# Second expert layer in three exact passes over 12-bit parts, weights in quarters of an expert, two attention units in turn

## The chip, the cores and the metric

The kernel runs on one core of a Trainium2 chip. In it TensorE does the matmuls, VectorE and ScalarE the work element by element, and transfers between device memory and the core's own memory are issued from DMA queues. The profile also records which share of its full clock TensorE was granted; in these traces that is full or half. The metric is the device time of the program in microseconds (us).

## The reference, cut to what matters

```python
q, k, v, alpha: (4 batches, 8 heads, 768 rows, 48)            # attention
for t in range(S):
    state = alpha[:, :, t, :, None] * state + einsum('bhd,bhe->bhde', k[:, :, t], v[:, :, t])
    y[:, :, t] = einsum('bhd,bhde->bhe', q[:, :, t], state)
x = y as (3072, 384)                                           # bridge
p = probs / (probs.sum(-1, keepdims=True) + 1e-09)             # 4 experts
for e in range(E):
    h = np.maximum(x @ w1[e], 0.0)                             # first layer, 384 -> 1024
    out += p[:, e:e + 1] * (h @ w2[e])                         # second layer, 1024 -> 384
```

## The kernel before

The attention is cut into 24 units of 128 rows. The experts run over seven groups of units: groups 0 and 1 have two units, groups 2 to 6 four. An "up" is 128 hidden columns of the first layer for one group; a "down" is the second layer of one expert for one unit. From group 1 on an up is exact through three cheap passes over parts of 12 bits: the high parts are multiplied, the low parts, and the differences of the two, and the mixed terms follow by subtraction. The parts of the weights are made once, in group 0, and kept in device memory. The second layer is in full precision:

```python
for out, parts in ((one, (1, 0)), (two, (2,))):        # up, groups 1 to 6
    for part in parts:
        for kc in range(KC):
            nc.tensor.matmul(out, lhsT=w1t[i][:, part, kc, col], rhs=xTs[gi][:, part, kc, :n], ...)
...
for fc in range(FCH):                                  # down: 8 matmuls in full precision
    nc.tensor.matmul(ops, lhsT=hidden[gi, e, h][:, f, slot * P:(slot + 1) * P], rhs=w2[:, fc, :], ...)
```

Weights come in halves of an expert. In group 0 a raw half, its scratch and its parts lie in different tiles, so no load waits for a store out of the same tile:

```python
t = staged[i] = wts.tile([P, KC, FH], F32, name="w_raw")     # raw half, two buffers
...
w = wts.tile([P, 3, KC, FH], F32R, name="w1")                # its parts, two buffers
... ScalarE and VectorE make the parts ...
nc.sync.dma_start(out=kept[i], in_=w.bitcast(F32))
```

## Time and profile before

| | before |
|---|---|
| time, median of 4 runs beside the changed kernel | 1339.6 us (1339.1 to 1342.6) |
| TensorE idle, from the trace | 51 us |
| half clock: half of the busy time inside the half-clock intervals of the clock record | 51 us, 17 of it in the start |
| the rest: TensorE's work at full clock | 1236 us |

The three rows below the time add up to the profiled span.

### The profile page before, as it was taken

Reading aid. Unit: us, or ns where it says so; the run is one execution under the profiler, and the core shown is the slowest. Engines: PE = TensorE matmul, PEld = TensorE weight load, DVE = VectorE, ACT = ScalarE, POOL = GpSimd, SP = SyncE. Lnnn points to the kernel's source line nnn. Section 1 sums busy time; section 2 is a strip of 40 time slices with the busy share of each in tenths; the row PEclk is TensorE's granted clock in tenths of the full one; section 3 lists DMA queues with packets and bytes.
Section 4 is the critical chain, followed back from the end, with each engine's and each line's share of the span. In section 5 each row is a group of like instructions: output and inputs, shape, how many; then the busy total and the mean of one; then the engine's idle time right before and its main releaser. Section 6 shows DMA issues by size and latency. Waiting matters only on the chain.

```text
span 1338.6 us, 18141 instructions
## 1 busy us (share of the span) xinstructions
PE 1287.5 (96%) x7288; PEld 944.0 (71%) x7288; DVE 600.5 (45%) x1320; ACT 324.2 (24%) x669; POOL 2.5 (0%) x14
## 2 busy tenths in 40 slices
PE   7999998899999999999999999999999999999998
PEld 6777777777777676676766776766767767656665
DVE  7456645543553553544544535535435435211221
ACT  1333311221232131231221321312312213211221
POOL 0000000000000000000000000000000000000000
PEclk7689988887999999999999999999999999999999
DMA  9188865553562452444533625524435325335430
GB/s 229 30 310 279 336 231 177 156 189 117 187 214 62 152 182 78 165 134 126 190 106 107 212 60 177 165 95 166 142 118 189 123 76 186 118 127 203 150 110 24
DMA packets 147138, 207.38 MB, mean 155 GB/s; under 512 B 104944, under 2 KB 136816, under 8 KB 139888
## 3 DMA queue, kind: packets, MB, share of 16 engines
q1 hardware_dynamic: 143680, 206.06, 46.2%
q8 instruction: 58, 0.95, 0.3%
q10 hardware_dynamic: 3376, 0.17, 0.2%
q14 instruction: 24, 0.20, 0.0%
HBM read 182.62 MB, written 23.59 MB: 154 GB/s over the span
## 4 chain that ended last, share of the span: by engine, by line
PE 90%; DVE 5%; ACT 3%; issue 1%; DMA 0%; SPq 0%; DVEq 0%; ACTq 0%
PE ops L353 39%; PE hps L328 27%; PE sc L221 11%; PE yps L256 3%; PE hps L311 3%; PE sc L218 3%; PE tp L179 2%; PE yps L253 1%; PE sps L267 1%; ACT t L333 1%; ACT AT L192 1%; DVE hT L334 1%; DVE lat L243 1%; ACT hT L338 1%; DVE acc L361 0%
## 5 line engine op out<-in xcount | busy, mean ns | idle before, releaser
L353 PE MATMUL ops<-w,hT 128*128 128x384 f32 x1536 | 524.7, 497 | 3.7 <-DVE acc L361 3.2
L353 PEld LDWEIGHTS ops<-w,hT 128*128 128x128 f32 x1536 | 289.2, 192 | 197.4 <-issue 6.9
L328 PE MATMUL hps<-xT,w 128*128 128x512 f32 (+1 forms) x1728 | 412.8, 389 | 4.6 <-DVE xT L295 4.0
L328 PEld LDWEIGHTS hps<-xT,w 128*128 128x128 f32 x1728 | 305.2, 194 | 63.0 <-DVE xT L295 4.5
L333 ACT ACTIVATE t<-hps 128x512 f32<-128x512 f32 (+1 forms) x192 | 107.7, 561 | 482.9 <-PE hps L328 482.8
L334 DVE TENSOR_TENSOR hT<-t,hps 128x512 f32<-128x512 f32 (+1 forms) x192 | 123.2, 642 | 165.9 <-ACT t L333 114.6
L221 PEld LDWEIGHTS sc<-QT,KT 48*128 48x128 f32 x1920 | 141.6, 209 | 58.5 <-issue 55.5
L361 DVE SCALAR_TENSOR_TENSOR acc<-ops,p_all,acc 128x384 f32<-128x384 f32 x72 | 44.5, 617 | 297.7 <-PE ops L353 297.7
L221 PE MATMUL sc<-QT,KT 48*128 48x64 f32 x1920 | 158.8, 300 | 12.7 <-DVE lat L243 12.6
L235 ACT COPY lat<-sc 32x128 f32<-32x128 f32 (+1 forms) x144 | 39.7, 292 | 359.8 <-PE sc L218 357.7
L243 DVE COPY_PREDICATED lat<-masks,sc 128x256 f32<-128x256 uint8 x240 | 116.6, 555 | 0.0
L338 ACT ACTIVATE hT<-hT 128x512 f32<-128x512 f32 (+1 forms) x192 | 112.9, 588 | 7.1 <-DVE hT L334 6.9
L227 DVE TENSOR_TENSOR QT<-QT,dec 128x256 f32<-128x256 f32 x144 | 61.2, 425 | 64.8 <-PE sc L221 56.4
L228 DVE TENSOR_TENSOR KT<-KT,dec 128x256 f32<-128x256 f32 x144 | 60.2, 418 | 0.0
L358 DVE TENSOR_SCALAR acc<-ops,p_all 128x384 f32<-128x384 f32 x24 | 14.8, 618 | 97.2 <-PE ops L353 97.2
L256 PE MATMUL yps<-rv,lat 128*128 128x48 f32 x384 | 56.4, 278 | 0.0
L256 PEld LDWEIGHTS yps<-rv,lat 128*128 128x128 f32 x384 | 52.9, 204 | 0.2
L311 PE MATMUL hps<-xT,w_raw 128*128 128x256 f32 x192 | 50.6, 414 | 0.6 <-ACT xT L288 0.6
L218 PEld LDWEIGHTS sc<-QT,KT 48*96 48x96 f32 (+1 forms) x768 | 34.2, 155 | 22.2 <-issue 19.4
L311 PEld LDWEIGHTS hps<-xT,w_raw 128*128 128x128 f32 x192 | 38.0, 206 | 7.5 <-ACT xT L288 1.0
L218 PE MATMUL sc<-QT,KT 48*96 48x64 f32 (+1 forms) x768 | 40.5, 246 | 2.1 <-DVE dec L230 1.9
L258 DVE TENSOR_TENSOR own<-own,yps 128x384 f32<-128x384 f32 x24 | 13.3, 554 | 46.9 <-PE yps L256 46.9
(53 smaller groups left out, 537.6 us busy)
## 6 DMA issues: line engine op xcount, KB each, us to landing
w<-kept SPq DMA_DIRECT2D x48, 2304.0 KB, 9.0
w<-in_moe_w_dram SPq DMA_DIRECT2D x28, 1536.0 KB, 7.0
kept<-w SPq DMA_DIRECT2D x8, 2304.0 KB, 8.0
w_raw<-in_moe_w_dram SPq DMA_DIRECT2D x8, 768.0 KB, 9.7
ra<-in_alpha_dram SPq DMA_DIRECT2D x24, 192.0 KB, 6.6
rk<-in_k_dram SPq DMA_DIRECT2D x24, 192.0 KB, 4.3
rq<-in_q_dram SPq DMA_DIRECT2D x24, 192.0 KB, 4.1
rv<-in_v_dram SPq DMA_DIRECT2D x24, 192.0 KB, 3.4
```

The lines of the kernel that those rows point to most:

```text
L218: nc.tensor.matmul(sc[i][:P - m, p, :], lhsT=KT[rows, p, :P - m], rhs=qv[rows, p, :, 1, :], start=True, stop=True)
L221: nc.tensor.matmul(sc[i][:, p, :], lhsT=KT[rows, p, :], rhs=qv[rows, p, :, 1, :], start=True, stop=True)
L227: nc.vector.tensor_mul(qv[:, :, :, 1, :], qv[:, :, :, 1, :], spread(left))
L228: nc.vector.tensor_mul(kv[:, :, :, 0, :], kv[:, :, :, 0, :], spread(right))
L243: nc.vector.copy_predicated(halves(lat[:, i], m)[:, :, :, 1, :], mk.unsqueeze(1).broadcast_to([P, NP, nb, m]), sc[i].rearrange("p a (b r) ...
L256: nc.tensor.matmul(yps[:, p, i, :], lhsT=lat[:, i, p, :], rhs=rv[:, 2 * p + i, :], start=(cb == 0), stop=(cb == 0 or i == 1))
L311: nc.tensor.matmul(out, lhsT=staged[i][:, kc, f * P:(f + 1) * P], rhs=xTs[gi][:, kc, :], start=(kc == 0), stop=(kc == KC - 1))
L328: nc.tensor.matmul(out, lhsT=w1t[i][:, part, kc, col], rhs=xTs[gi][:, part, kc, :n], start=(part == parts[0] and kc == 0), stop=(part == p ...
L333: nc.scalar.activation(out=t, in_=one, func=ACT.Copy, scale=1 + 1 / 4096.0)
L334: nc.vector.tensor_sub(hT, t, two)
L338: nc.scalar.activation(out=r, in_=r, func=ACT.Relu)
L353: nc.tensor.matmul(ops, lhsT=hidden[gi, e, h][:, f, slot * P:(slot + 1) * P], rhs=w2[:, fc, :], start=(fc == 0), stop=(fc == FCH - 1))
```

## The change

The intent is to put the second layer, the dearest group of the profile, through the same three passes. Each down then has 24 cheap matmuls instead of 16 instructions of full precision. For that the hidden values and the second-layer weights need parts too. The weights of both layers now lie in quarters of an expert, and the parts are made in the buffer that the raw quarter was loaded into. There are four buffers for the second layer and three for the first. The attention is dealt out by estimated time, two units in turn. The order changes too: the kernel before runs the downs of one expert between the two halves of the next expert's ups, and the changed kernel runs all ups of an expert and then its downs.

```diff
+    split1 = lambda gi, e: gi > 0
+    split2 = lambda gi, e: gi > 1 or gi == 1 and e < E // 2
+    makes = {0: lambda gi, e: gi == 0,
+             1: lambda gi, e: gi == 0 and e < E // 2 or gi == 1 and e >= E // 2}
 [...]
+    def load_piece(l, i):
+        w = wt[l][i] = wts.tile([P, 3, KC * QF], F32R, name=f"w{l + 1}", bufs=3 if l == 0 else NQ)
+        if (split1, split2)[l](gi, e):
+            nc.sync.dma_start(out=w.bitcast(F32), in_=kept[l][k])
+        elif l == 0:
+            nc.sync.dma_start(out=w[:, 2]..., in_=moe_w1[e]...)
 [...]
+    def split_piece(l, i):                        # in place: the raw quarter lies in part 2
+        nc.scalar.activation(out=top, in_=dif.bitcast(F32), func=ACT.Copy, scale=TRIM)
+        nc.vector.tensor_sub(low.bitcast(F32), dif.bitcast(F32), top.bitcast(F32))
+        nc.scalar.activation(out=low, in_=low.bitcast(F32), func=ACT.Copy, scale=4096.0)
+    def keep_piece(l, i):
+        nc.vector.tensor_sub(dif, top.bitcast(F32), low.bitcast(F32))
+        nc.sync.dma_start(out=kept[l][i % (E * NQ)], in_=w.bitcast(F32))
 [... up: the hidden values are split too ...]
+            nc.vector.tensor_sub(t, t, two)
+            finish.append(split(t, parts, relu=True))      # ScalarE once, VectorE twice
 [... down ...]
+                nc.tensor.matmul(sums[0], lhsT=h[:, 1], rhs=w[:, 1], start=(fc == 0), stop=False)
+                nc.tensor.matmul(sums[0], lhsT=h[:, 0], rhs=w[:, 0], start=False, stop=(fc == FCH - 1))
+                nc.tensor.matmul(sums[1], lhsT=h[:, 2], rhs=w[:, 2], **ends)
 [... attention ...]
+                turn = waiting.pop(0)
+                if next(turn, waiting) is not waiting:
+                    waiting.insert(min(1, len(waiting)), turn)
+                    due -= 1.0
```

## The prediction

> **What bounds the kernel now.** I read the page's first two parts, the groups, the table of stretches and then the timelines. The program runs 24 attention units of 128 rows and an expert layer over seven groups of them: groups 0 and 1 hold two units, groups 2 to 6 four. While a group's experts run, TensorE also does the attention of the next group. Group boundaries below are the starts of each group's first matmul of the first layer.
>
> ```profile
> PE 1287.5 (96%) x7288; PEld 944.0 (71%) x7288; DVE 600.5 (45%) x1320; ACT 324.2 (24%) x669; POOL 2.5 (0%) x14
> PEclk7689988887999999999999999999999999999999
> DMA  9188865553562452444533625524435325335430
> ```
>
> The reader is to see that TensorE sets the time, and that the first quarter differs: there its clock is granted in part and the DMA engines are busiest. The table of stretches says it by stage (columns: length; busy us of each engine; granted clock; DMA share; GB/s):
>
> ```profile
> 0.00:52.00 52.00, 43.00 (x311) 39.33 (x311) 30.30 (x80) 9.06 (x21) 2.53 (x14) 0.65 0.61 152
> 52.00:165.00 113.00, 105.59 (x600) 80.01 (x601) 69.85 (x115) 41.55 (x68) 0.00 (x0) 0.95 0.77 273
> 165.00:341.00 176.00, 159.27 (x1070) 127.30 (x1070) 83.01 (x213) 36.60 (x103) 0.00 (x0) 0.84 0.52 174
> 540.00:750.00 210.00, 207.53 (x1196) 149.67 (x1197) 97.20 (x220) 49.00 (x102) 0.00 (x0) 0.99 0.42 137
> 1163.00:1338.00 175.00, 170.05 (x609) 114.33 (x607) 35.01 (x53) 37.39 (x67) 0.00 (x0) 1.00 0.37 131
> ```
>
> Group 3 (540 to 750) is TensorE and nothing else; DVE has 97 of 210 us. The costliest groups:
>
> ```profile
> L353 PE MATMUL ops<-w,hT 128*128 128x384 f32 x1536 | 524.7, 497 | 3.7 <-DVE acc L361 3.2
> L328 PE MATMUL hps<-xT,w 128*128 128x512 f32 (+1 forms) x1728 | 412.8, 389 | 4.6 <-DVE xT L295 4.0
> L361 DVE SCALAR_TENSOR_TENSOR acc<-ops,p_all,acc 128x384 f32<-128x384 f32 x72 | 44.5, 617 | 297.7 <-PE ops L353 297.7
> ```
>
> Of the second layer, 768 matmuls of the program are 1536 instructions. What one costs is read where nothing is mixed in, in the chain of waits of the last group, which has no attention (start, us, what):
>
> ```profile
> 1232.00 16.50 PE hps L328 x72
> 1248.50 20.64 PE ops L353 x64
> ```
>
> 64 instructions of 384 columns in 20.64 us are 322.5 ns each, so one row block of one expert ("down") costs 16 x 322.5 = 5.16 us. 72 reduced-precision matmuls of 512 columns in 16.50 us are 229 ns each, so one slice of 128 hidden columns ("up") costs 9 x 229 = 2.06 us. For 256 columns (group 1) the trace has 116 to 120 ns from start to start inside a run.
>
> **What the Trainium skill says.** "FP8 and Floating Point Precision", TensorE Precision Notes: "True FP32: 4 passes through PE array". The trace agrees: two instructions of 322.5 ns for 384 columns, and 2 x 384 cycles at the 2.4 GHz that "TensorE: Matmul & The Clock Gate" names are 320 ns. "VectorE: DVE Perf Modes", the perf-mode tier table: a two-tensor fp32 operation stays at 1x. It agrees: 128x512 took 686 ns, 128x256 422 ns, 128x1536 1756 ns, about 1.04 ns an element and 155 ns besides. "DMA: Bandwidth & Descriptors", Anatomy of one DMA: semaphore waits happen on the issuing sequencer, not in the DMA engines, so one wait holds everything issued behind it. The trace agrees: the waits of the DMA queue include 295.3 us of first-layer weight loads waiting for TensorE. "TensorE: Matmul & The Clock Gate", HAM oscillation: idle gaps over about 3.4 us return the array to half clock. The clock record of this trace knows only full and half, 106 us of half in all, 55 of them in group 1.
>
> **The change part by part.**
>
> *Second layer in three passes.* From group 2 on, and for two experts of group 1, a down becomes 24 single-instruction matmuls of 384 columns. No row shows that size; between 118 ns (256) and 229 ns (512) lies 173.5 ns, so 4.17 us. The saving is 0.99 us for each of 80 + 4 downs: 83 us, all on the path of TensorE. This is the whole direct gain, 6.2%.
>
> *What it adds on DVE.* Hidden values must be split: to the one subtraction of an up come two more two-tensor operations, 3 x 0.69 = 2.07 us an up against TensorE's 2.06. Each down has two accumulations of 0.617 us in place of one. So DVE is full in the up phases before any attention. From the built order I counted, in each up phase of eight, the attention work that stands in it, by the durations of the trace. TensorE then has 24.3, 26.3, 24.3 and 20.5 us in the four experts' up phases of a steady group; DVE has 32.3, 20.5, 31.8 and 23.5 us. PSUM (four banks, two for an up) lets TensorE lead by about two ups. At the end the split of the last slices must be finished before the first down reaches its last quarter, about 3.5 us in; DVE ends about 2.7 us after its own sum because of the first up and the first activation. So the stalls are 32.3 + 2.7 - 24.3 - 3.5 = 7, none, 7 less what the tail pieces give back, and 2: I take 13 us a group in groups 3 and 4, 10 in group 2, 15 in group 5, 3 in group 6, together 54. In the down phases DVE has about 13 of 23 us.
>
> *What it moves in DMA.* Second-layer parts are kept too: 24 stores of 1152 KB in group 0 (16 first layer, 8 second) and 8 in group 1. The parts now lie in the load's own buffer. So a load into it waits for the store out of it, and while the DMA queue waits for that nothing behind is issued. In the trace a store of 2304 KB has its first packet 0.8 us after issue, 8 packets of 0.80 us an engine, and lands 0.4 us later (8.0 in all). Half of it is 0.8 + 3.2 + 0.4 = 4.4 us. With the next load (384 KB, 1.1 us) ahead of the next store, a cycle is 5.45 us; with a load of 1152 KB (3.0 us by 0.37 us a packet) 7.3 us. First-layer weights have three buffers for four quarters. The fourth quarter of an expert therefore waits for the store of the first, and after an expert whose second layer was kept, that store stands behind four such cycles, 22 us. TensorE gets through three quarters in 10 to 12 us. Walking the queue's order with these numbers, group 0 stalls by 3, 14, 16 and 3 us (36); group 1 by 10 (three stores and four loads of group 0's end lie ahead), 2, 4 (this one DVE) and 16 (32); the first expert of group 2 by 17 (four cycles of 7.3 us, attention inputs, then its quarter). From then on the loads of an expert (4.7 MB, 11.8 us) and the fourth quarter (3.0) land about 14 us into an up phase of 24 that needs it after 18: hidden.
>
> *Attention dealt by time, two units in turn.* It takes away waits of TensorE for the attention chain, and by itself helps group 1, which now loses 22 us to gaps and 26 to half clock.
>
> **The sum.** TensorE's work at full clock after the change, from the built order and these durations: start 51, group 0 113, group 1 125, groups 2 to 4 186.5 each, group 5 177, group 6 133, together 1158. The same tally for the kernel before is 83 more, 1241, of its 1339; the other 98 are idle time (51, from the page) and half clock (about 50). After: 1158 + 36 + 32 + 17 for DMA + 54 for DVE + 22 for half clock after the long stalls (two thirds of what is lost now would be 33; some hides inside the stalls) = **1319 us**, 1.5% less.
>
> **Rivals.** (a) *TensorE stays the only bound*: the two units in turn hide DVE, the stores land earlier than I reckon, and of 83 us some 70 are kept and group 1 gains 20 more: about 1250. For it: before the change DVE delays TensorE by 3 us in the down groups; the down phases have DVE time to spare. Against it: DVE's 32 us in an up phase of 24, and no bank for TensorE to lead further. (b) *The DMA queue takes the start over entirely*: the stalls in groups 0 to 2 add a half clock each time and attention loads wait in the same queue: 1360 to 1380. For it: the DMA share in group 0 is already 0.77, and the bytes of groups 0 and 1 grow from some 60 to over 80 MB. (c) *DVE sets steady groups too*: more attention waits on a late DVE, a steady group stays at 208 as now; then 1319 + 20.
>
> **Range and chances.** The direct gain is certain within 10 us (the 384-column spacing). The DMA stalls are 85 with an error of 25, DVE's 54 with 20, the clock 22 with 15. Together some 37, so 1268 to 1366. My own sum stands just above the limit of 2% (1313), hence faster 0.44, same 0.46, slower 0.10; the last is (b).
>
> **What would show it.** In the changed profile: second-layer matmuls spaced 174 ns; steady groups about 200 us with DVE over 70% busy and waits of TensorE for the hidden tiles in the first and third expert; in groups 0 to 2 waits of TensorE for DMA into the first-layer weights of 10 to 17 us each, about six of them, each followed by half clock; no DMA wait after group 2. I am wrong if group 0 takes under 130 us, or steady groups take 188, or if DMA waits go on to the end.

## More of the kernel before

One more view of this kernel, the waits of TensorE (what waited and for what; us in total, times, longest):

```profile
PE tp L179 <- ACT AT L192: 14.8, 21, 2.0
PE sc L221 <- DVE lat L243: 12.6, 15, 2.2
PE tp L179 <- DMA ra<-in_alpha_dram: 4.2, 2, 3.6
```

TensorE's longest wait is 3.6 us, and it never waits for a weight.

## The result, and the profile after

The changed kernel takes 1420.4 us (median of 4 runs, 1417.3 to 1428.4) against 1339.6: slower by 6.1%, ratio 1.0607 with a 95% interval of 1.056 to 1.0655. Ratios here are the mean time of one kernel's fast runs over that of the other's fast runs of the same rounds, so they are not quite the ratio of the medians quoted. All outputs are right. The prediction, 1319 us, was wrong, and its range, up to 1366, did not hold the result.

First the page of the changed kernel, the lines that answer to the three at the head of the prediction:

```profile
PE 1254.8 (88%) x7960; PEld 1090.6 (77%) x7960; DVE 850.5 (60%) x1744; ACT 376.5 (27%) x759; POOL 2.5 (0%) x14
PEclk7677879578576879999999999999999999999999
DMA  6276466957335765647655735846466575367663
```

TensorE has less to do, 1254.8 us for 1287.5, and the span is 81 us longer. The loss lies in the first 15 of the 40 slices, 533 us, where the clock is granted in part. The table of stretches puts figures on it (columns as in the prediction; group 0, 1, 2, a steady group, the last group):

```profile
54.00:257.00 203.00, 135.80 (x686) 101.58 (x686) 85.15 (x157) 60.18 (x110) 0.00 (x0) 0.79 0.61 212
257.00:461.00 204.00, 170.09 (x1058) 149.45 (x1059) 99.02 (x241) 51.72 (x123) 0.00 (x0) 0.70 0.57 199
461.00:688.00 227.00, 198.26 (x1334) 174.37 (x1333) 142.77 (x296) 56.34 (x113) 0.00 (x0) 0.93 0.61 206
688.00:888.00 200.00, 196.09 (x1328) 173.28 (x1327) 140.17 (x291) 55.33 (x111) 0.00 (x0) 0.97 0.60 210
1276.00:1420.00 144.00, 133.81 (x672) 120.34 (x670) 81.68 (x126) 38.54 (x68) 0.00 (x0) 1.00 0.62 245
```

A steady group takes 200 us where it took 210: that part of the change works. Group 0 takes 203 where 113 were needed before, and group 1 takes 204 for 176. The waits of TensorE in the changed kernel:

```profile
PE one L343 <- DMA w<-kept: 50.2, 7, 22.9
PE one L335 <- DMA w<-in_moe_w_dram: 47.5, 4, 19.4
PE sc L241 <- DVE lat L254: 26.0, 15, 6.7
PE sc L238 <- ACT lat L247: 10.8, 19, 3.8
```

The first two did not exist before: the first layer waits for its weights. There are four such waits in group 0 (5.3, 19.4, 16.7 and 6.2 us), a long one in group 1 (20.0) and one in the first expert of group 2 (22.9), 90.5 us together; five more, 0.9 to 2.4 us, stand in group 6. The other two are attention; four of these, 3.4 to 6.7 us, fall in the downs of group 0. There the chain's own VectorE and ScalarE work stands behind the making of weight parts.

The chain of work that ended last, in the stretch of the 19.4 us wait (start, us, what):

```profile
98.91 8.05 DMA kept<-w
...
107.49 6.08 DMA kept<-w
...
114.08 5.89 DMA kept<-w
...
120.48 5.76 DMA kept<-w
...
126.29 4.75 DMA w<-in_moe_w_dram
```

The reader sees four stores one behind the other, the four second-layer quarters of the first expert. Behind them stands the load of the first-layer quarter that TensorE is waiting for. The load into a quarter's buffer must wait for the store out of it, and the DMA queue issues nothing past that wait.

The account of the two traces, by my sum over the matmuls and the clock record (us; idle / half clock / work at full clock):

| | before | after |
|---|---|---|
| whole span | 51 / 51 / 1236 | 165 / 105 / 1150 |
| group 0 of the changed kernel | | 67 / 22 / 114 |
| group 1 | | 34 / 50 / 120 |
| group 2 | | 29 / 5 / 193 |
| group 3 | | 4 / 5 / 191 |

So 86 us of TensorE's work are gone, and they are given back by 114 us more idle time and 53 us more half clock.

### The profile page after: what moved, and what is told of

The parts are those of the page before. It is cut to its first block, busy times and chain, and to the rows that moved or that the text cites. A ratio compares the mean times of both kernels' runs of the same rounds, so it can differ in the third digit from the quotient of the medians.

```text
span 1420.0 us, 20156 instructions
## 1 busy us (share of the span) xinstructions
PE 1254.8 (88%) x7960; PEld 1090.6 (77%) x7960; DVE 850.5 (60%) x1744; ACT 376.5 (27%) x759; POOL 2.5 (0%) x14
## 4 chain that ended last, share of the span: by engine, by line
PE 69%; DVE 13%; DMA 11%; ACT 2%; issue 2%; SPq 1%; DVEq 0%; ACTq 0%
PE one L343 14%; PE ops L390 9%; PE ops L391 8%; PE ops L393 8%; PE sc L241 7%; PE two L343 6%; DMA kept<-w 5%; DMA w<-kept 4%; DVE lat L254 3%; PE yps L275 3%; PE sc L238 3%; PE one L335 3%; PE ops L395 3%; PE tp L197 2%; PE yps L272 2%
## 5 line engine op out<-in xcount | busy, mean ns | idle before, releaser
L343 PE MATMUL one<-xT,w 128*128 128x512 f32 (+1 forms) x1152 | 304.6, 403 | 50.4 <-DMA w<-kept 50.2
L343 PEld LDWEIGHTS one<-xT,w 128*128 128x128 f32 x1152 | 210.2, 203 | 91.0 <-issue 48.0
L347 ACT ACTIVATE t<-one 128x512 f32<-128x512 f32 (+1 forms) x192 | 108.1, 563 | 548.5 <-PE one L343 481.5
L390 PE MATMUL ops<-w,hT 128*128 128x384 f32 x672 | 236.1, 351 | 0.0
L393 PE MATMUL ops<-w,hT 128*128 128x384 f32 x672 | 230.3, 343 | 0.0
L391 PE MATMUL ops<-w,hT 128*128 128x384 f32 x672 | 230.1, 342 | 0.0
L349 DVE TENSOR_TENSOR t<-t,two 128x512 f32<-128x512 f32 (+1 forms) x176 | 116.3, 661 | 101.0 <-PE two L343 74.0
L343 PE MATMUL two<-xT,w 128*128 128x512 f32 (+1 forms) x576 | 161.1, 391 | 0.0
L343 PEld LDWEIGHTS two<-xT,w 128*128 128x128 f32 x576 | 111.6, 205 | 20.5
L179 DVE SCALAR_TENSOR_TENSOR hT<-hT 128x512 fp32r<-128x512 f32 (+1 forms) x176 | 117.5, 668 | 6.1
L175 DVE SCALAR_TENSOR_TENSOR hT<-t,hT 128x512 fp32r<-128x512 f32 (+1 forms) x176 | 116.0, 659 | 0.0
L172 ACT ACTIVATE hT<-t 128x512 fp32r<-128x512 f32 (+1 forms) x176 | 106.3, 604 | 9.6 <-DVE t L349 9.6
L335 PEld LDWEIGHTS one<-xT,w 128*128 128x128 f32 x192 | 44.9, 243 | 58.0 <-issue 31.5
```

Source lines behind the costliest of these rows:

```text
L172: nc.scalar.activation(out=top, in_=x, func=ACT.Relu if relu else ACT.Copy, scale=TRIM)
L175: nc.vector.scalar_tensor_tensor(out=low, in0=x, scalar=0.0, in1=top.bitcast(F32), op0=ALU.max, op1=ALU.subtract)
L179: nc.vector.scalar_tensor_tensor(out=dif, in0=top.bitcast(F32), scalar=1 / 4096.0, in1=low.bitcast(F32), op0=ALU.mult, op1=ALU.subtract)
L335: nc.tensor.matmul(one, lhsT=w[:, 2, kc].bitcast(F32), rhs=xraws[gi][:, kc, :n], start=(kc == 0), stop=(kc == KC - 1))
L343: nc.tensor.matmul(out, lhsT=w[:, part, kc], rhs=xTs[gi][:, part, kc, :n], start=(part == terms[0] and kc == 0), stop=(part == terms[-1] a ...
L347: nc.scalar.activation(out=t, in_=one, func=ACT.Copy, scale=FINE)
```

## The experiments

Three theories. A: the DMA queue and the missing fourth buffer of the first layer. B: in group 1 the mix of short matmuls keeps the clock at half after it has once fallen. C: attention held behind the weights' making on VectorE and ScalarE. The rival to all of them was the plain sum of bytes and VectorE work, whatever its order. A table of all stages follows the last run; medians of the kernel before were 1337.7 to 1338.0 us.

**Second-layer transfers on a queue of their own.**

```diff
-            nc.sync.dma_start(out=w.bitcast(F32), in_=kept[l][k])
+            (nc.sync, nc.gpsimd)[l].dma_start(out=w.bitcast(F32), in_=kept[l][k])
   (the raw second-layer load and the store likewise)
```

> All loads and stores of second-layer weights are issued from GpSimd's queue instead of SyncE's; nothing else changes. Theory A (TensorE's long waits for a first-layer quarter come from the one in-order DMA queue, where the second layer's store-then-load cycles stand ahead; and these waits set off most of the half clock): the seven waits over 5 us (sum about 114 us in the changed kernel) fall to under 40 us, busy time at half clock in groups 0 to 2 falls from 155 us to under 90, total about 1310 to 1330. Theory B (the waits cost only themselves; the half clock of group 1 comes from its mix of 256-column ups with small attention matmuls): idle falls by the same 60 to 75 us, but group 1 still has about 80 to 100 us busy at half clock, total 1345 to 1360. Theory C (the splits of weights in the in-order queues of ScalarE and DVE hold everything up): waits hardly change, total within 20 us of 1420.

1411.0 us, ratio 1.055 (1.0508 to 1.0592). The first-layer waits shrink: 5.5, 11.1, 12.7 and 6.0 us in group 0, 5.1 in group 1, none in group 2. In their place TensorE waits for second-layer quarters, 6.5 + 4.0 us in group 1 and 8.4 + 7.1 in group 2. Idle falls by 20 us, half clock rises by 10. By the medians the order in one queue is worth 9 us, not 80, and the two intervals overlap. By time this is the branch of theory C, though the waits did change. The edit also changes the kind of queue: the page of this run has 132 MB under a software queue, where the changed kernel has almost all under one hardware queue.

**The second layer in full precision everywhere.**

```diff
-    split2 = lambda gi, e: gi > 1 or gi == 1 and e < E // 2
+    split2 = lambda gi, e: False
-             1: lambda gi, e: gi == 0 and e < E // 2 or gi == 1 and e >= E // 2}
+             1: lambda gi, e: False}
```

> The second layer stays in full precision everywhere, no parts of it are made, stored or loaded; quarters, attention by time and the two units in turn stay. Its matmuls cost 84 x 0.99 = 83 us more. Theory A: without second-layer stores the waits for quarters shrink to under 25 us in all and the half clock to the level of the kernel before (some 65 us busy at half), total about 1335, i.e. the kernel before again. Theory B: waits go too, but group 1 keeps half clock in its ups (80 us busy at half or more), total about 1365 to 1385. Theory C: like A for the waits; TensorE's waits for attention in group 0's down phases (19 us) go as well.

1373.4 us, ratio 1.0267 (1.0219 to 1.0314). Without its three-pass second layer the change is still 2.7% slower than before; the first-layer waits of group 0 are then 4.2 to 6.1 us each. So the second layer in parts costs another 47 us net, and 36 come from the rest. The time lies in the range of theory B, but its reason does not hold here. Group 1:

```profile
210.00:364.00 154.00, 144.43 (x1031) 117.36 (x1030) 72.03 (x191) 39.42 (x108) 0.00 (x0) 0.89 0.60 195
```

Its ups and its attention are those of the changed kernel, and theory B expected 80 us or more of busy time at half clock there; 33 us were recorded. The half clock costs group 1 16 us here, 50 in the changed kernel and 26 in the kernel before.

**Ups of group 1 run twice** (the same result written again).

```diff
-            for out, terms in ((one, (1, 0)), (two, (2,))):
+            for out, terms in ((one, (1, 0)), (two, (2,))) * (2 if gi == 1 else 1):
```

> In group 1 alone each up runs its nine matmuls twice (the second run overwrites the first, the result is the same): 288 more matmuls of 118 ns, 34 us at full clock, 68 at half. Theory A (waits set off the half clock): group 1 gets longer by 34 to 60 us, total 1450 to 1480. Theory B (too little dense work between attention pieces keeps the clock at half): the up phases of group 1 run at full clock (3.1 us a slice instead of 4.1), busy time at half clock in group 1 falls from 100 us to under 50, and in spite of more work the total is 1385 to 1420.

1429.5 us, ratio 1.0676 (1.0644 to 1.0708). TensorE gets 37 us more work at full clock in group 1, yet the stage grows only from 204.5 to 209.0 us. The stretch of group 1 in this run:

```profile
257.00:466.00 209.00, 176.86 (x1348) 159.61 (x1348) 99.06 (x242) 52.23 (x124) 0.00 (x0) 0.88 0.55 194
```

The granted clock rises from 0.70 to 0.88 and the busy time at half clock falls from 101 to 39 us. Much of group 1's time is the low clock, which long runs of matmuls lift: that part of theory B holds. Its range for the time, 1385 to 1420, was missed by 9 us. Two stretches of group 1 in the changed kernel show what it looks like (after the length: busy us of TensorE; the first 0.50 is the clock):

```profile
253.00:294.00 41.00, 39.14 (x218) 36.31 (x219) 26.47 (x71) 5.62 (x16) 0.00 (x0) 0.50 0.86 298
342.00:379.00 37.00, 36.60 (x209) 32.61 (x208) 19.77 (x54) 6.76 (x18) 0.00 (x0) 0.50 0.46 162
```

TensorE is recorded busy for 95 and 99% of these stretches and stays at half clock for 41 and 37 us. The matmuls of 256 columns in them come 214 ns apart, against 116 to 120 ns at full clock, so the record is right here. Between the ups stand bursts of 16 attention matmuls of 64 columns.

**The parts made just before their store instead of ahead of use.**

```diff
     def keep_piece(l, i):
+        split_piece(l, i)
   (the two earlier calls of split_piece are taken out)
```

> Each weight quarter is split into its parts just before its store, not ahead of the matmuls that use it whole; the matmuls of these stages don't need the parts. Theory C: TensorE's waits for attention in group 0's down phases (6.7, 4.8, 3.5, 3.4 us) go, with the half clock after them: total 1385 to 1400. Theory A: the stores start some us later for it (two more operations of about 0.85 us each ahead of each), the waits for quarters stay or grow, total 1415 to 1435.

1415.6 us, ratio 1.0575 (1.0536 to 1.0614); idle 158, half clock 106. Two of the attention waits grew, to 12.1 and 10.9 us, and the waits for quarters shrank from 98 to 76 us in sum. Theory C isn't refuted as a cost, since the attention waits only moved, but moving the making brings 5 us by the medians, with intervals that overlap.

**A fourth buffer for first-layer quarters.**

```diff
-        w = wt[l][i] = wts.tile([P, 3, KC * QF], F32R, name=f"w{l + 1}", bufs=3 if l == 0 else NQ)
+        w = wt[l][i] = wts.tile([P, 3, KC * QF], F32R, name=f"w{l + 1}", bufs=NQ)
-            load_piece(0, i + 2)
+            load_piece(0, i + 3)
   (and i + NQ for i + 3 after a quarter's last use; four loads at the start)
```

> First-layer quarters get a fourth buffer, so the fourth quarter of an expert needn't wait for the store of the first; stores and everything else as in the changed kernel. If the missing buffer itself makes the waits: the four waits of group 0 (5, 19, 17, 6 us), the 20 us of group 1 and the 23 us of group 2 fall below 15 us in sum, total about 1330 to 1350. If the sheer chain of eight store-and-load cycles an expert (about 44 us against 28 us of TensorE's work) makes them: the waits of experts without second-layer stores go (5 and 6 us), the long ones only move to the next expert's first quarters, total 1395 to 1415.

1349.2 us, ratio 1.0077 (1.0041 to 1.0114): 71 us less than the changed kernel from one buffer. The first branch of the expectation, the missing buffer itself, is the one that came true. Its stretches (groups 0, 1, 2 and 3):

```profile
53.00:225.00 172.00, 136.20 (x686) 99.45 (x686) 85.06 (x157) 58.41 (x110) 0.00 (x0) 0.82 0.67 230
225.00:408.00 183.00, 163.77 (x1062) 143.00 (x1063) 97.88 (x240) 52.33 (x124) 0.00 (x0) 0.76 0.68 242
408.00:620.00 212.00, 198.64 (x1334) 174.93 (x1333) 144.36 (x298) 55.80 (x113) 0.00 (x0) 0.96 0.65 223
620.00:819.00 199.00, 195.17 (x1322) 172.54 (x1321) 139.38 (x290) 55.27 (x111) 0.00 (x0) 0.97 0.60 210
```

And its two longest sums of waits of TensorE:

```profile
PE ops L395 <- DMA w<-in_moe_w_dram: 26.7, 7, 4.5
PE sc L241 <- DVE lat L254: 23.0, 15, 6.9
```

No first-layer wait is left in the list. What waits for DMA is now the second layer, in pieces of at most 4.5 us there and 6.9 at group 2. Idle falls from 165 to 97 us. The half clock stays, 102 us for 105: it is not merely the shadow of the waits.

**The second layer's parts made in groups 2 and 3 instead of 0 and 1.**

```diff
-    split2 = lambda gi, e: gi > 1 or gi == 1 and e < E // 2
+    split2 = lambda gi, e: gi > 3 or gi == 3 and e < E // 2
-             1: lambda gi, e: gi == 0 and e < E // 2 or gi == 1 and e >= E // 2}
+             1: lambda gi, e: gi == 2 and e < E // 2 or gi == 3 and e >= E // 2}
```

> Parts of the second layer are made and stored in groups 2 and 3 (two experts each) in place of groups 0 and 1, and used from then on; 28 downs stay at 5.16 us instead of 4.17, which costs TensorE 28 us. If the stores in the short groups are what hurts: idle time of groups 0 and 1 falls from 101 to about 37 us and half clock there to the 32 us lost of the run with the whole second layer; groups 2 and 3 hide most of the stores (waits of about 5 us each in four experts); total 1335 to 1355. If the stores cost the same wherever they stand: idle moves to groups 2 and 3 (60 us or more there), total 1400 or more.

1415.3 us, ratio 1.0584 (1.0547 to 1.0621). The waits move with the making: group 2 takes 256 us and group 3 takes 234, and over the whole run TensorE waits 48.0 us for kept first-layer quarters (longest 15.0). So little is gained by moving the making while a buffer is missing: idle falls by 27 us and half clock by 8, and 24 us of second-layer work in full precision come in their place.

**The same with the fourth buffer, and the first layer's parts made half in group 0, half in group 1.**

```diff
+    split1 = lambda gi, e: gi > 1 or gi == 1 and e < E // 2
+    makes = {0: lambda gi, e: gi == 0 and e < E // 2 or gi == 1 and e >= E // 2,
+             1: lambda gi, e: gi == 2 and e < E // 2 or gi == 3 and e >= E // 2}
   (group 1 keeps its raw x in a tile of its own, and there is one buffer less for the sums, acc)
```

> As the last one, with the fourth buffer, and the first layer's parts made half in group 0, half in group 1 (its third and fourth expert stay in full precision there, 3.5 us more of TensorE). The accounts of the runs so far add up to: work at full clock 1150 + 28 + 4, idle 40 to 60, lost to half clock 50 to 65: total 1275 to 1310, which would beat the kernel before (1338). If groups 2 and 3 don't hide the stores: 1320 to 1350.

1354.1 us, ratio 1.0122 (1.0088 to 1.0157). Group 0 falls to 122 us, and groups 2, 3 and 4 take 243, 224 and 210. Both expected ranges, up to 1350, were missed. Against the run with the fourth buffer, idle and half clock fall by 27 us together, and the 29 us more work on TensorE, in full precision until the parts are made, take that back.

**One attention unit after the other**, on the changed kernel.

```diff
-                    waiting.insert(min(1, len(waiting)), turn)
+                    waiting.insert(0, turn)
```

> The changed kernel with one attention unit after the other, as before the change; the dealing by time stays. If two units in turn take away waits as intended, their absence adds waits of TensorE for VectorE in the chain of levels, in the steady groups about 5 to 15 us each: total 1440 to 1480. If it makes no difference, VectorE's delay in these groups being hidden anyway: 1410 to 1430.

1495.5 us, ratio 1.1174 (1.1131 to 1.1217), more than the 1440 to 1480 expected; a steady group takes 215 us instead of 199. Two units in turn are worth 75 us in this kernel. That doesn't say that the kernel before, with its other order, would gain from it.

**One layer's parts at a time, with the fourth buffer.**

```diff
-    split1 = lambda gi, e: gi > 0
-    split2 = lambda gi, e: gi > 1 or gi == 1 and e < E // 2
-    makes = {0: lambda gi, e: gi == 0,
+    split1 = lambda gi, e: gi > 1 or gi == 1 and e >= E // 2
+    split2 = lambda gi, e: gi > 1
+    makes = {0: lambda gi, e: gi == 0 and e >= E // 2 or gi == 1 and e < E // 2,
   (the fourth buffer, raw x of group 1 and acc as two runs above)
```

> The fourth first-layer buffer (as in the run with it), and each expert now makes the parts of one layer at a time: group 0 makes the second layer of experts 0 and 1 and the first layer of experts 2 and 3, group 1 the other way round, so four stores of 1152 KB an expert instead of eight. The second layer in parts begins with group 2 for all experts. Theory A (too many stores and loads in the queue within an expert of group 0 hold the second-layer pieces back): group 0 falls from 172 us to about 135, group 1 from 183 to about 175, the rest as with the fourth buffer alone (work about 8 us more), in all 1290 to 1315 us, faster than before. Rival (what remains in groups 0 and 1 is the sum of bytes, whatever their order): groups 0 and 1 together stay at 350 us and the time at 1345 to 1360.

1344.6 us, ratio 1.0048 (1.003 to 1.0065). Group 0 falls from 172 to 146 us, most of what was expected. Group 1 rises from 183 to 188, group 2 from 212 to 218 and group 5 from 191 to 198. So what was expected, faster than before, was missed: groups 0 and 1 together are 21 us shorter in the profiled runs, and all but 3 of them come back later. Theory A holds for group 0 alone.

**The same with every up of group 1 in full precision.**

```diff
-    split1 = lambda gi, e: gi > 1 or gi == 1 and e >= E // 2
+    split1 = lambda gi, e: gi > 1
```

> As the run with one layer each, but the ups of experts 2 and 3 of group 1 are in full precision too, so that no 256-column reduced-precision matmuls stand in group 1. About 4 us more work. Theory B (the mix of short matmuls keeps the clock at half in group 1): the half-clock loss of group 1 falls below 10 us, and the time is 10 to 25 us under that of the run with one layer each. Rival (the clock falls because of the waits alone): the loss stays within 5 us of that run's and the time is equal or 4 us more.

1327.1 us, ratio 0.9908 (0.9878 to 0.9938), the only version that beats both kernels; but 0.9% is under the 2% from which a difference counts here. Group 1 in the run with one layer each:

```profile
199.00:387.00 188.00, 162.20 (x1002) 126.36 (x999) 95.58 (x214) 57.25 (x122) 0.00 (x0) 0.82 0.65 224
```

And in this run:

```profile
200.00:374.00 174.00, 156.13 (x950) 118.41 (x951) 89.49 (x198) 52.58 (x108) 0.00 (x0) 0.88 0.61 207
```

Group 1 has 5 us more work and takes 14 less: half clock falls by 11 us (29 to 18) and idle time by 8. The gain of 17 us is what theory B said, but the half clock did not fall below 10, and the mix of matmuls is not all that changed: VectorE has 6 us less to do in this group, and the DMA share falls from 0.65 to 0.61.

**The second layer in full precision, with the fourth buffer** (the edit of the second run on top of the fifth).

> The second layer in full precision everywhere, nothing of it made or stored, with the fourth first-layer buffer. If the buffer is missed only because second-layer stores are queued ahead of it, this is the run with the whole second layer again less the 20 us of first-layer waits left there: 1345 to 1355 us. Then the second layer's 86 us of saved work are all given back in the run with the fourth buffer (1349), by making and by VectorE. If the buffer is worth 70 us here too: about 1300 us, and the three-pass second layer is a loss of 50.

1343.5 us, ratio 1.0047 (1.0027 to 1.0066). It is as fast as the run with parts and the same buffers, 1349.2, or 6 us faster. So even with enough buffers the three passes bring nothing net. By stage, in the profiled runs, the parts save 13 to 15 us in each of groups 3 to 5, 16 in group 6 and 9 in group 2, some 65 in all; they cost 45 us in group 0 and 23 in group 1.

**One VectorE operation of the hidden split done twice**, on the run with the fourth buffer.

```diff
+        for _ in range(2 if relu else 1):
             nc.vector.scalar_tensor_tensor(out=dif, in0=top.bitcast(F32), scalar=1 / 4096.0, ...)
```

> With the fourth first-layer buffer; the last VectorE operation of the split of the hidden values is done twice (same result), 0.69 us more VectorE an up with 512 columns, 160 of them, 110 us in all and no TensorE work. If VectorE sets the up phases of the first, third and fourth expert, as predicted: 15 to 17 us more in each of groups 2 to 5, about 20 in group 6, together 75 to 90 us more than the run with the fourth buffer (1425 to 1440). If TensorE alone sets the steady groups: at most 15 us more (under 1365).

1445.6 us, ratio 1.0811 (1.0778 to 1.0844): 96 us more for about 110 us more VectorE work, and nothing more on TensorE. A steady group:

```profile
626.00:851.00 225.00, 210.59 (x1325) 181.70 (x1324) 161.21 (x322) 55.22 (x111) 0.00 (x0) 0.92 0.53 186
```

VectorE has 22 us more than in the run with the fourth buffer (139.4), and the group grows by 25; in the account of the two stretches 12 us more are half clock, 11 idle time and 3 work. So VectorE is at its limit in the steady groups although it is busy only 70% of them in the changed kernel: what is added to it lands on the time. That it already held the group up by much does not follow, and no run took work away from it alone. In the changed kernel's timeline one round of an up phase shows why (VectorE alone: start, us, instruction):

```profile
702.21 0.68 DVE L349 TENSOR_TENSOR t<-t,two 128x512 f32<-128x512 f32 x1
702.80 0.68 DVE L175 SCALAR_TENSOR_TENSOR hT<-t,hT 128x512 fp32r<-128x512 f32 x1
703.52 0.69 DVE L179 SCALAR_TENSOR_TENSOR hT<-hT 128x512 fp32r<-128x512 f32 x1
704.13 1.30 DVE L254 COPY_PREDICATED lat<-masks,sc 128x256 f32<-128x256 uint8 x2
705.23 0.45 DVE L262 TENSOR_TENSOR QT<-QT,dec 128x256 f32<-128x256 f32 x1
705.60 0.41 DVE L263 TENSOR_TENSOR KT<-KT,dec 128x256 f32<-128x256 f32 x1
705.92 0.28 DVE L265 TENSOR_TENSOR dec<-dec 128x128 f32<-128x128 f32 x1
706.13 0.68 DVE L349 TENSOR_TENSOR t<-t,two 128x512 f32<-128x512 f32 x1
```

There is no gap: one up and one attention level take 3.9 us of VectorE, for 2.06 us of the up's matmuls and about 1.1 us of the attention's (16 at a median spacing of 71 ns). Yet hardly a wait is recorded on TensorE. The gaps between first-layer matmuls are no wider than in the kernel before: median 230 ns and a tenth over 315 in this group, 231 and 315 in group 3 before. The attention's score matmuls are: from start to start they take 35.8 us in this group for 28.3 before. But they take 33.6 us in the run with the second layer whole and four buffers, so some 5 us of that are there without the parts, and about 2 come with them.

**All stages together** (length in us; the kernel before overlaps the ups of one expert with the downs of the one before, so its boundaries lie a little otherwise; numbers of the profiled runs):

| stage | before | after | second layer whole | whole, 4 buffers | parts, 4 buffers | one layer each | group 1 full precision | one more operation |
|---|---|---|---|---|---|---|---|---|
| start | 52 | 54 | 53 | 53 | 53 | 54 | 54 | 53 |
| group 0 | 113 | 203 | 157 | 127 | 172 | 146 | 146 | 171 |
| group 1 | 176 | 204 | 154 | 159 | 183 | 188 | 174 | 183 |
| group 2 | 199 | 227 | 217 | 220 | 212 | 218 | 219 | 220 |
| group 3 | 210 | 200 | 211 | 213 | 200 | 203 | 202 | 225 |
| group 4 | 209 | 198 | 214 | 216 | 201 | 201 | 201 | 225 |
| group 5 | 204 | 190 | 207 | 204 | 191 | 198 | 194 | 209 |
| group 6 | 176 | 144 | 153 | 153 | 137 | 138 | 139 | 158 |

## Why the prediction was wrong

By the steps of its sum, in us. The waits for quarters are those of TensorE for first-layer weights, half clock is counted outside the start, and "other idle" stands against the 54 put down to VectorE:

| term | predicted | measured |
|---|---|---|
| start | 51 | 54 |
| TensorE's work at full clock in the groups | 1107 | 1125 |
| waits for first-layer quarters | 36 + 32 + 17 = 85 | 48 + 20 + 23 = 91 |
| VectorE / other idle | 54 | 62 |
| half clock after the long stalls | 22 | 88 |
| sum | 1319 | 1420 |

*The direct gain* was right: the second-layer matmuls come 174 ns apart where 173.5 was worked out, and 86 us of work are gone for 83.

*The tally of work* was short before the change as well: outside the start it gives 1190 us for the kernel before, where the trace has 1211. Its check (1241 + 98 = 1339) came out because the 9 us of idle time and 17 of half clock in the start were counted in both numbers. And the 22 us that group 1 was said to lose to gaps are 17 in the trace.

*The steady groups* had the right length: 199.8 and 198.0 us for 199.5, 189.7 for 192, VectorE at 70%; group 6 took 144 for 136. That VectorE is at its limit there was right: one operation more put 25 us on a group, where my own sum had 16 of them on the path. What it costs was not. The sum charged 13 us a group, as waits for the hidden tiles that the trace doesn't show. With four buffers the parts save 13 and 15 us in groups 3 and 4, of the 16 that the matmuls alone save, which leaves 1 to 3 for VectorE. The rest of the 13 was there before the change: the tally gives 202 us for group 3 of the kernel before, which took 210. So the length came out partly by luck, and so did the row of 54 and 62: only 29 of the 62 us fall in groups 2 to 6.

*The waits for quarters* were right in cause and sum: predicted 3, 14, 16 and 3 in group 0, measured 5.3, 19.4, 16.7 and 6.2; of 10, 2, 4 and 16 in group 1 only the last came, as 20.0; 17 in group 2 were 22.9. The four stores shown took 5.8 to 8.1 us for the 4.4 worked out, which holds for a store with nothing ahead of it (4.2 us for the first one). The fourth buffer shows the cause; what it saves, 71 us, is most of the 91. The other part comes back as waits of the second layer for its quarters. One sign of being wrong came true in a small way: five waits of 7.4 us in all stand in group 6, where none was foreseen after group 2.

*The step that failed* is "22 for half clock after the long stalls": it is 88 us, 22 in group 0 and 50 in group 1. I had taken the half clock as a tail of each stall. The trace shows 41 and 37 us in a row with TensorE busy, and the second began with no long wait, only a stretch of 4 us in which TensorE was busy for 3. The run with the fourth buffer takes the long stalls for first-layer quarters away and keeps the half clock, 102 us. The run with the ups done twice and the run with group 1 in full precision both raise the clock; the first adds 37 us of work for 4.5 us of time, the second shortens the stage. What brings the clock down is only narrowed. The ups and attention of group 1 are the same in three runs that leave its second layer whole, and there it costs 16 us (without the fourth buffer), 28 (with it) and 28 (parts made in groups 2 and 3); with the second layer's parts made and used in group 1 it costs 50, and 42 with the fourth buffer. So the mix of ups and attention alone accounts for a third to two thirds, and the rest comes with the second layer's parts in this group, by a way that no run shows.

*Left out altogether* were 33 us of other idle time in groups 0 and 1 (19 and 14; the kernel before has 7 and 17 us idle there), mostly attention held behind the making of parts on VectorE and ScalarE. No run took these waits away alone; the run that moved the making only moved them. That the second layer's parts as a whole cost 45 and 23 us in these groups is shown by the pair of runs with four buffers.

*The rivals.* That the DMA queue takes the start over (1360 to 1380) was nearest, and given a chance of 0.10; it was still 40 us short, because it too charged the half clock by the stall.

*Where the gain went*: from the kernel before, the change with four buffers and the second layer whole costs 6 us; the three passes gain some 65 us in groups 2 to 6 and lose 68 in groups 0 and 1, and by the two medians 6 on balance; the missing buffer costs 71. *Open*: why steady groups with the second layer whole take 213 to 216 us in the new order instead of 210 (5 us of it lie in the attention's score matmuls), and what exactly keeps the clock down in group 1, since no run varied the mix one kind of matmul at a time.

## What to carry to other kernels

Count the buffers of a piece that is loaded, changed in place and stored again against the pieces used in one pass: one buffer short put a store and a load between two matmuls here, and cost 71 us. A change that saves time in steady stages by work done in the first ones must be charged for those: 68 us lost in groups 0 and 1 ate a gain of 65. When a stage has stalls and short matmuls together, charge the clock for the whole stage and not for a tail of each stall; and test whether an engine is at its limit by adding one operation to it and seeing if the time follows. Before a view is taken as the mark of a stall, look at the same view of the kernel before.

## What the Trainium skill lacked or had wrong

- "TensorE: Matmul & The Clock Gate", What's actually happening, has the array back at full clock after about 3.4 us of sustained activity. Here it stayed at half for 41 and 37 us while recorded busy for 95 and 99% of them, in a mix of 256-column and 64-column matmuls (spacing 214 ns at 256 columns, for 116 to 120 at full clock). The page does tell of a clock that swings where TensorE pauses often and briefly between groups of matmuls; it has no rule by which to say whether a mix like this one counts as such.
- The same page, Seeing it yourself, warns that the clock events of a trace can be unreliable. In two runs the record gives 1.00 for the start, where matmuls come 213 ns apart as in the runs whose record says half there, against 112 ns for the same line at full clock.
- No page has the spacing of reduced-precision fp32 matmuls: 116 to 120 ns at 256 columns, 174 at 384, 229 at 512.
